# A recurrent token mixer and a token MLP on one core: from two loops over batch and head pair to planned units of 256 tokens

## The chip, the cores and the metric

The kernel runs on one core of one Trainium2 chip. The metric is the device time of one execution in microseconds (us); the number compared is the median of the runs. The core has TensorE (matrix products, into PSUM), VectorE, ScalarE, GpSimd and SyncE, and 16 transfer (DMA) engines. In the profile they are PE (with PEld for the loading of its stationary operand), DVE, ACT, POOL and SP.

## The reference

Inputs are fp32: r, k, v, w of shape batch 4, heads 8, tokens 768, head width 48; u of 8 x 48; and three small matrices. The first part is a recurrence per batch and head with a 48 x 48 state, the second mixes the tokens of a batch.

```python
for t in range(S):
    cur = einsum('bhd,bhe->bhde', u * kt, vt)
    y[:, :, t] = einsum('bhd,bhde->bhe', rt, state + cur)
    state = wt[..., None] * state + einsum('bhd,bhe->bhde', kt, vt)
x = y as (B, S, 384)                      # heads side by side
wq = x @ w_q; wk = x @ w_k                # 384 -> 64
W_tok = 64 ** -0.5 * einsum('bsd,btd->bst', wq, wk)
out = relu(einsum('bst,btd->bsd', W_tok, x)) @ w_out
```

Both kernels cut the recurrence into chunks of 128 tokens. In a chunk the decays become exponentials of running sums of logarithms of w; the tokens of a chunk act on each other through a masked 128 x 128 product per head, earlier chunks through the state. Both compute the mixing as wq (wk^T x), so that no 768 x 768 matrix arises.

## The kernel before

There are two loops: over the 4 batches, and within a batch first over 4 head pairs (`prep`), then over 6 chunks of 128 tokens (the scan), then the mixer. The order of instructions on each engine is that of the text; a tile framework adds the waits, and tiles with several buffers let a batch run into the next.

`prep` loads w, k, r and v of one head pair for all 768 tokens (four transfers of 288 KB on SP's queue, in pieces of 192 bytes, three buffers each). ScalarE takes the logarithm (`logw`, L144), TensorE sums along the tokens by triangular matrices (`cw`), ScalarE takes two exponentials (`ecwx`, L151, and `emcw`, L158), VectorE and GpSimd multiply r and k by them (`RdS`, L166, and `KdS`, L168). TensorE transposes both into `psT`, VectorE copies that to `RKT` (L177). Products `A` of 48 rows follow per chunk and head, and VectorE masks them into `AmB` (L188). The diagonal term with u is two products on GpSimd (`uk`, L195 and L196), a sum on VectorE (L198) and a product on GpSimd (`Vd`, L199). The scan makes a new state per chunk (`Sn`, then `SB`, L238) and the output `Y`, to which VectorE adds `Vd` (`X`, L250); each second chunk is transposed into `XT` (ScalarE copy, L260). The mixer has `wk_s`, `wqT`, `Tps`, six `mps` with a relu on ScalarE (L288), and six `fps` with a copy on VectorE (`osb`, L296) and a store on SP's queue (L297).

PSUM tiles of the scan, of the mixer and of the column sums `ptp` (L162, made in `prep`) share one ring `m` of two buffers:

```python
def mtile(shape, dtype, name):
    return ps.tile(shape, dtype, name=name, tag="m", bufs=2)
```

All matrix products go through the helper at L53, so that TensorE's instructions have line 54.

Of the kernel before, what the change touches and what calls it, by code (L numbers as in the profile page):

```python
# [18 lines left out]
def _rep(ap, axis, n):  # L19
    a = [list(x) for x in ap.ap]  # L20
    a.insert(axis, [0, n])
    return dataclasses.replace(ap, ap=a)
# [3 lines left out]
def kernel(  # L26
# [14 lines left out]
    C = 128  # L41
    NCH = S // C
# [5 lines left out]
    scale = 1.0 / math.sqrt(DH)  # L48

    MU = -0.13468  # L50
    LN_SCALE = math.exp(-MU)

    def mm(o, l, rr, start=True, stop=True, sgc=True, trans=False):  # L53
        nc.tensor.matmul(o, l, rr, start=start, stop=stop,  # L54
                         skip_group_check=sgc, is_transpose=trans)
# [4 lines left out]
    U128 = consts.tile([C, C], BF16, tag="U128")  # L60
    make_upper_triangular(nc, U128, 1.0, diag=True)
    US128 = consts.tile([C, C], BF16, tag="US128")
    make_upper_triangular(nc, US128, 1.0, diag=False)
    ID128 = consts.tile([C, C], BF16, tag="ID128")
    make_identity(nc, ID128)
    ones = U128[:, C - 1:C]

    iota0 = consts.tile([C, 1], mybir.dt.int32, tag="iota0")
    nc.gpsimd.iota(iota0, pattern=[[0, 1]], base=0, channel_multiplier=1)
    iota1 = consts.tile([C, 1], mybir.dt.int32, tag="iota1")  # L70
    nc.gpsimd.iota(iota1, pattern=[[0, 1]], base=1, channel_multiplier=1)
    bias_px = consts.tile([C, 1], F32, tag="bpx")
    bias_mi = consts.tile([C, 1], F32, tag="bmi")
    bias_c = consts.tile([C, 1], F32, tag="bc")
    nc.scalar.activation(bias_px, iota0, ACT.Copy, bias=0.0, scale=MU)
    nc.scalar.activation(bias_mi, iota1, ACT.Copy, bias=0.0, scale=-MU)
    nc.gpsimd.memset(bias_c, MU * C)

    NB = 3
    LW = []
    RdS = []
    for i in range(NB):
        t = consts.tile([C, NCH, C], BF16, name=f"logw{i}", tag=f"logw{i}")
        nc.gpsimd.memset(t, 0.0)
        LW.append(t)
        t = consts.tile([C, NCH, C], BF16, name=f"RdS{i}", tag=f"RdS{i}")
        nc.gpsimd.memset(t, 0.0)
        RdS.append(t)  # L90
    KdS = []
    PT = []
    for i in range(2):
        t = consts.tile([C, NP, NCH, C], BF16, name=f"KdS{i}", tag=f"KdS{i}")
        nc.vector.memset(t, 0.0)
        KdS.append(t)
        t = consts.tile([C, NCH, H], F32, name=f"pt{i}", tag=f"pt{i}")
        nc.vector.memset(t, 0.0)
        PT.append(t)

    u1 = consts.tile([1, DM], F32, tag="u1")
    ubc = consts.tile([C, DM], F32, tag="ubc")
    wq_sb = consts.tile([128, NK, DH], BF16, tag="wq")
    wk_sb = consts.tile([128, NK, DH], BF16, tag="wk")
    wout_sb = consts.tile([128, NK, DM], BF16, tag="wo")
    wq_f = consts.tile([128, NK, DH], F32, tag="wqf")

    ld = ctx.enter_context(tc.tile_pool(name="ld", bufs=3))
    hw = ctx.enter_context(tc.tile_pool(name="hw", bufs=3))
    bt = ctx.enter_context(tc.tile_pool(name="bt", bufs=2))  # L110
    sm = ctx.enter_context(tc.tile_pool(name="sm", bufs=3))
    ps = ctx.enter_context(tc.tile_pool(name="ps", bufs=1, space=bass.MemoryType.PSUM))
    xpool = ctx.enter_context(tc.tile_pool(name="xpool", bufs=2))
    msb = ctx.enter_context(tc.tile_pool(name="msb", bufs=2))
    mout = ctx.enter_context(tc.tile_pool(name="mout", bufs=4))

    def mtile(shape, dtype, name):
        return ps.tile(shape, dtype, name=name, tag="m", bufs=2)

    def prep(b, hp, AmB, RKT, VB, Vd, ptp):  # L120
        n = b * NP + hp
        wG = ld.tile([C, 2 * NCH, D], F32, name="wG", tag="wG")
        kG = ld.tile([C, 2 * NCH, D], F32, name="kG", tag="kG")
        rG = ld.tile([C, 2 * NCH, D], F32, name="rG", tag="rG")
        vG = ld.tile([C, 2 * NCH, D], F32, name="vG", tag="vG")
        for ap, tl in ((w, wG), (k, kG), (r, rG), (v, vG)):
            nc.sync.dma_start(out=tl, in_=ap[b, ds(hp * 2, 2)].rearrange(  # L127
                "h (c p) d -> p (h c) d", p=C))
        if n == 0:
            nc.sync.dma_start(out=u1, in_=u.rearrange("h d -> (h d)"))  # L130
            nc.gpsimd.partition_broadcast(ubc, u1)

        def hcd(t):
            return t.rearrange("p (h c) d -> p h c d", h=2)

        def chd(t):
            return t.rearrange("p (h c) d -> p c h d", h=2)

        def pad(t):
            return t.rearrange("p c (h x) -> p c h x", h=2)[:, :, :, 0:D]  # L140

        logw = LW[n % NB]
        for hh in range(2):
            nc.scalar.activation(logw[:, :, ds(hh * 64, D)],  # L144
                                 wG[:, ds(hh * NCH, NCH)], ACT.Ln,
                                 bias=0.0, scale=LN_SCALE)
        cw1 = ps.tile([C, 2, 512], F32, name="cw1", tag="cw")
        for hh in range(2):
            mm(cw1[:, hh, 0:NCH * D], US128, logw[:, :, ds(hh * 64, D)])
        ecwx = hw.tile([C, 2, NCH, D], BF16, name="ecwx", tag="ecwx")  # L150
        nc.scalar.activation(ecwx.rearrange("p h c d -> p h (c d)"),  # L151
                             cw1[:, :, 0:NCH * D], ACT.Exp,
                             bias=bias_px, scale=1.0)
        cw0 = ps.tile([C, 2, 512], F32, name="cw0", tag="cw")
        for hh in range(2):
            mm(cw0[:, hh, 0:NCH * D], U128, logw[:, :, ds(hh * 64, D)])
        emcw = hw.tile([C, 2, NCH, D], BF16, name="emcw", tag="emcw")
        nc.scalar.activation(emcw.rearrange("p h c d -> p h (c d)"),  # L158
                             cw0[:, :, 0:NCH * D], ACT.Exp,
                             bias=bias_mi, scale=-1.0)  # L160
        for c in range(NCH):
            mm(ptp[:, hp, ds(c, 1)], logw[:, c], ones)  # L162
# [165 lines left out]
```

## Time and profile before

| | |
|---|---|
| median of 3 runs | 181.64 us (180.85 to 182.18) |
| profiled execution, its span | 182.1 us (no other time is given for it) |
| TensorE, weight loads | 121.0 us, 74.3 us |
| VectorE | 112.7 us |
| ScalarE | 74.0 us |
| GpSimd | 95.3 us |
| TensorE's granted clock, mean | 0.869 of full speed |
| moved by transfers | 24.23 MB in 104,000 packets |

The span runs from the first to the last instruction of the profiled execution. Busy time of an engine is the time in which it worked on at least one instruction; the rest it waited or had nothing left.

### The profile page before, as it was taken

What the parts mean: (1) busy time and instruction counts of PE and PEld (TensorE: products, weight loads), DVE (VectorE), ACT (ScalarE), POOL (GpSimd) and SP (SyncE); (2) the same over time, 40 slices, a digit from 0 to 9 for tenths busy, and PEclk for the clock granted to TensorE, in tenths of its full rate; (3) what the DMA queues carried; (4) which work ended last, traced back from release to release, by engine and by line L of the source; (5) the groups of instructions that cost most, each with busy time, mean ns of one, the idle gap of its engine ahead of it and who ended that gap; (6) DMA issues with size and microseconds to landing.
All of it is one profiled execution on the core that took longest, in us unless ns stands there. A gap on an engine that the chain in (4) does not pass through costs nothing.

```text
span 182.1 us, 3121 instructions
## 1 busy us (share of the span) xinstructions
PE 121.0 (66%) x1200; PEld 74.3 (41%) x1200; DVE 112.7 (62%) x156; ACT 74.0 (41%) x140; POOL 95.3 (52%) x86
## 2 busy tenths in 40 slices
PE   0152178130698787966988986688888964787791
PEld 0121045010465653343765533465564243565240
DVE  6011147469889977644799778179996553744042
ACT  3175473310045446066346461944456232022620
POOL 8410599999728976406993954379586202000000
PEclk9999999999999997585599999657999697557969
DMA  7999999999999300399999908999940240000024
GB/s 127 186 188 187 187 185 158 196 215 157 169 187 168 67 4 2 142 236 200 190 178 191 166 13 237 235 168 200 185 73 0 86 150 27 0 5 0 0 81 178
DMA packets 104000, 24.23 MB, mean 133 GB/s; under 512 B 100529, under 2 KB 103986, under 8 KB 103986
## 3 DMA queue, kind: packets, MB, share of 16 engines
q1 hardware_dynamic: 103186, 23.70, 76.7%
q0 software_dynamic: 800, 0.34, 1.5%
q8 instruction: 9, 0.15, 0.4%
q14 instruction: 5, 0.04, 0.1%
HBM read 19.66 MB, written 4.72 MB: 134 GB/s over the span
## 4 chain that ended last, share of the span: by engine, by line
PE 25%; DVE 23%; issue 18%; POOL 12%; ACT 7%; DMA 7%; SPq 6%; POOLq 1%; ACTq 0%; DVEq 0%
DVE RdS L166 6%; PE psT L54 6%; DVE X L250 5%; SPq L127 5%; DVE RKT L177 5%; POOL uk L196 4%; DMA wG<-in_w_dram 3%; ACT XT L260 3%; POOL uk L195 3%; PE cw L54 3%; POOL Vd L199 3%; PE wq_ps L54 2%; PE fps L54 2%; DVE AmB L188 2%; PE Tps L54 2%
## 5 line engine op out<-in xcount | busy, mean ns | idle before, releaser
L168 POOL TENSOR_TENSOR KdS<-kG,emcw 128x576 bf16<-128x576 f32 x16 | 22.2, 1388 | 41.5 <-ACT emcw L158 33.2
L188 DVE TENSOR_TENSOR AmB<-A,US 128x768 bf16<-128x768 f32 x32 | 30.4, 950 | 5.7 <-PE A L54 4.4
L166 DVE TENSOR_TENSOR RdS<-rG,ecwx 128x576 bf16<-128x576 f32 x16 | 20.8, 1298 | 20.2 <-ACT ecwx L151 14.6
L177 DVE COPY RKT<-psT 128x1536 bf16<-128x1536 bf16 x16 | 15.3, 953 | 19.4 <-PE psT L54 19.3
L195 POOL TENSOR_TENSOR uk<-kG,ubc 128x576 f32<-128x576 f32 x16 | 24.0, 1499 | 0.0
L196 POOL TENSOR_TENSOR uk<-uk,rG 128x576 f32<-128x576 f32 x16 | 23.6, 1476 | 0.6
L199 POOL TENSOR_TENSOR Vd<-VB,diag 128x576 bf16<-128x576 bf16 x16 | 18.7, 1172 | 8.4 <-ACT VB L170 6.2
L54 PE MATMUL A<-RKT 48*128 48x128 bf16 x192 | 17.5, 263 | 7.0 <-DVE RKT L177 4.2
L144 ACT ACTIVATE logw<-wG 128x288 bf16<-128x288 f32 x32 | 12.4, 435 | 23.7 <-PE ptp L54 11.3
L151 ACT ACTIVATE ecwx<-cw,bias_px 128x576 bf16<-128x576 f32 x16 | 11.9, 741 | 24.6 <-PE cw L54 24.5
L54 PEld LDWEIGHTS <-KdS 128*128 128x128 bf16 x176 | 16.1, 123 | 13.7 <-POOL KdS L168 9.9
L54 PEld LDWEIGHTS <-RKT 48*128 48x128 bf16 (+1 forms) x272 | 13.6, 108 | 19.6 <-issue 9.3
L54 PE MATMUL fps<-wout_sb,mixT 128*128 128x384 bf16 x72 | 19.7, 418 | 1.7 <-ACT mixT L288 1.2
L296 DVE COPY osb<-fps 128x384 f32<-128x384 f32 x24 | 13.0, 554 | 12.4 <-PE fps L54 12.2
L54 PE MATMUL cw<-logw,US 128*128 128x288 bf16 x32 | 10.5, 365 | 13.4 <-ACT logw L144 12.9
L260 ACT COPY XT<-xt_ps 128x768 bf16<-128x768 bf16 x12 | 9.6, 799 | 21.4 <-PE xt_ps L54 21.4
L158 ACT ACTIVATE emcw<-cw,bias_mi 128x576 bf16<-128x576 f32 x16 | 11.9, 742 | 11.3 <-PE cw L54 11.2
L54 PE MATMUL psT<-ID,RdS 128*128 128x128 bf16 x96 | 11.4, 272 | 7.5 <-DVE RdS L166 7.5
L54 PE MATMUL cw<-logw,U 128*128 128x288 bf16 x32 | 9.7, 386 | 8.4 <-ACT ecwx L151 8.4
L54 PE MATMUL psT<-ID,KdS 128*128 128x128 bf16 x96 | 12.7, 277 | 2.8 <-POOL KdS L168 2.8
L170 ACT CAST VB<-vG 128x576 bf16<-128x576 f32 x16 | 10.7, 666 | 7.8 <-DMA vG<-in_v_dram 7.7
L54 PE MATMUL Sn<-VB,KdS 128*128 128x96 bf16 x80 | 9.9, 238 | 5.4 <-POOL KdS L168 5.4
(53 smaller groups left out, 181.1 us busy)
## 6 DMA issues: line engine op xcount, KB each, us to landing
wG<-in_w_dram SPq DMA_DIRECT2D x16, 288.0 KB, 5.6
kG<-in_k_dram SPq DMA_DIRECT2D x16, 288.0 KB, 5.3
rG<-in_r_dram SPq DMA_DIRECT2D x16, 288.0 KB, 5.6
vG<-in_v_dram SPq DMA_DIRECT2D x16, 288.0 KB, 5.6
out_dram<-osb SPq DMA_DIRECT2D x24, 192.0 KB, 1.9
wout_sb<-in_moe_w_out_dram POOLq DMA_DIRECT2D x1, 288.0 KB, 4.8
wq_f<-in_moe_w_q_dram SPq DMA_DIRECT2D x1, 96.0 KB, 4.6
wk_sb<-in_moe_w_k_dram POOLq DMA_DIRECT2D x1, 48.0 KB, 4.6
```

The source lines that it names most:

```text
L54: nc.tensor.matmul(o, l, rr, start=start, stop=stop, skip_group_check=sgc, is_transpose=trans)
L144: nc.scalar.activation(logw[:, :, ds(hh * 64, D)], wG[:, ds(hh * NCH, NCH)], ACT.Ln, bias=0.0, scale=LN_SCALE)
L151: nc.scalar.activation(ecwx.rearrange("p h c d -> p h (c d)"), cw1[:, :, 0:NCH * D], ACT.Exp, bias=bias_px, scale=1.0)
L166: nc.vector.tensor_tensor(pad(Rd), chd(rG), ecwx.rearrange("p h c d -> p c h d"), ALU.mult)
L168: nc.gpsimd.tensor_tensor(pad(Kd), chd(kG), emcw.rearrange("p h c d -> p c h d"), ALU.mult)
L177: nc.vector.tensor_copy(RKT[:, hp], psT[:, :, 0:NCH * C])
L188: nc.vector.tensor_tensor(AmB[:, ds(hp * 2, 2), ds(g * NG, NG)], A[:, :, 0:NG * C].rearrange("p h (c t) -> p h c t", c=NG), _rep(_rep(US12 ...
L195: nc.gpsimd.tensor_tensor(uk, hcd(kG), _rep(ubs, 2, NCH), ALU.mult)
L196: nc.gpsimd.tensor_tensor(uk, uk, hcd(rG), ALU.mult)
L199: nc.gpsimd.tensor_tensor(Vd[:, :, ds(hp * 2, 2)], VB[:, :, ds(hp * 2, 2)], _rep(diag.rearrange("p h c -> p c h"), 3, D), ALU.mult)
L260: nc.scalar.copy(XT[:, :, ds((c - 1) * C, 2 * C)], tp)
L296: nc.vector.tensor_copy(osb, fps)
```

## The change

The work is cut into 12 units, each of 256 tokens of one batch over all 8 heads. A unit is a list of some 50 steps, each with an engine, a booked duration, a rank, the steps it comes after and the buffer it fills. A scheduler in the kernel's text (`Plan.order`) plays these through at build time, with at most three transfers queued and PSUM as eight banks that are given out and taken back, and writes the steps in the order in which they came to start. The ranks are a unit number times 100 plus written-out offsets (`OFF`, `DEL`); a table (`ENG`) says per unit which of ScalarE (A), VectorE (D) and GpSimd (P) does a copy or product.

The parts change as well. A load brings 256 tokens of all heads in one transfer (393 KB, pieces of 384 bytes: two neighbouring tokens lie in one partition). k and r are cast to bf16 (`k16`, `r16`) and transposed by TensorE as they are; the running sums come out transposed (`cw`), and the exponentials `en` and `ep` are applied after the transposes: `RT` on VectorE out of PSUM, `KT` on VectorE or GpSimd. `kb` and `kd` turn `KT` back for the state. The diagonal term is a VectorE product `qT`, eight TensorE products with u as two columns (`dps`), a small copy (`dd`), and `Vd` on GpSimd. V is cast on GpSimd with the token pairs still side by side (`v16`); four transfers within SBUF put it in chunk order (`VB`). Masks take 1024 columns at a time. Copies of the mixer take a unit at a time: `xts`, `qks`, relu, `os`. The output is stored once a unit, 256 tokens. In the first and the last unit some steps are split in halves, and in the last the store of the first half is issued by ScalarE. Products of a zero tile stand at the start (9, and 26 as filler steps) and before the last batch's mixing (16).

The diff, cut to its core:

```diff
...
+    def add(self, eng, dur, rank, fn, after=(), fill=None, read=(), lag=100, mode=0,
+            behind=None, leave=0):
...
+    def dma(self, issue, dur, rank, fn, after=(), fill=None, read=()):
+
+        i = self.add("SP", issue, rank, fn, after, fill, read, lag=0)
+        m = self.add("DQ", dur, 0, self.nothing, [i], lag=0)
+        return i, self.add(f"L{m['n']}", 1950, 0, self.nothing, [m], lag=0)
...
+        ready = [s for s in self.steps if not left[s["n"]]]
+        running, done, eng_free, now = [], [], {}, 0
+        mode = queued = 0
+        while ready or running:
+            ready.sort(key=lambda s: (s["rank"] - self.stick * (s["eng"] == "PE"
+                                                                and s["mode"] == mode), s["n"]))
+            started = True
+            while started:
...
+                    if s["behind"] is not None and "start" not in s["behind"]:
+                        continue
+                    if ready_at[s["n"]] > now or eng_free.get(s["eng"], 0) > now:
+                        continue
+                    if s["eng"] == "SP" and queued >= 3:
+                        continue
...
+    U = 2 * C
+    NU = S // U
...
+    PS = ps.tile([C, 4096], F32, name="PS", tag="PS")
...
+    def load(b, i, tl, ap):
+        nc.sync.dma_start(
+            out=view(tl, 0, [[D2, H], [1, D2]]),
+            in_=ap[b, :, ds(i * U, U)].rearrange("h (p j) d -> p h (j d)", j=2))
...
+    for _ in range(9):
+        mm(PS[:, ds(0, 512)], Z[:, ds(0, C)], Z)
...
+    ENG = dict(k16="AAAAAPPPPPPP", r16="DADPPADPPPPA", KT="PDPDPPPPPPPP", kd="DAAADDDADAAA",
+               xts="ADDDDAADDDAA", qks="AADAAADAAAAA", rl="AAAAAAAAAAAA", os="AAAAAAAAAAAD",
+               dd="DADDDDDDDAAA", ks="AAAAAAAAAADA")
+    DEL = dict(load=[-2909, -1987, -122, 0, 5, 4, 16, 68, 52, 0, 4, 229],
...
+               os=[-209, -40, -196, 108, 0, 0, -5, -37, -26, 82, -198, -60],
...
+    kinds = {"os": NOS, "SB": 3}
+    for name in ("wg", "rg", "kg", "vg"):
+        kinds[name] = NB
+    for name in ("lw", "r16", "k16", "ep"):
+        kinds[name] = 2
+    for name in ("en", "ks", "qT", "RT", "KT", "ptm", "v16", "VB", "dd", "Vd", "AM0", "AM1", "KD", "XT"):
+        kinds[name] = NS
+    kinds["MX"] = 4
...
+    def warm(count, dur, after=()):
+
+        def f():
+            mm(stile(F32, "warm"), Z[:, ds(0, C)], Z)
+        for _ in range(count):
+            s_ = plan.add("PE", dur, 1 << 20, f, after, fill="s", lag=0)
+            plan.reads(s_, s_, True)
...
+        def f_cw():
+            t["cw"] = cw = wtile("cw")
+            for hp in range(NP):
+                for j in range(2):
+                    for c in range(2):
+                        mm(cw[:, ds(c * 512 + hp * C, C)],
+                           lw[ds(c * 64, 64), ds(j * 512 + hp * 128, 128)],
+                           CM[ds(c * 64, 64), ds(j * C, C)],
...
+            def f_en(cs=cs):
+                nc.scalar.activation(sb("en", [C, 1024])[:, cols(cs, 512)],
+                                     t["cw"][:, cols(cs, 512)], ACT.Exp, bias=0.0, scale=-1.0)
...
+        def f_qT():
+            nc.vector.tensor_tensor(sb("qT", [C, 1024]), t["rT"], t["ks"], ALU.mult)
...
+                nc.vector.tensor_tensor(
+                    view(sb("RT", [C, 1024]), cs[0] * 512, [[C, n4], [64, 2], [1, 64]]),
+                    view(t["rT"], cs[0] * 512, [[C, n4], [64, 2], [1, 64]]),
+                    view(ep, cs[0] * NP * EW, [[EW, n4], [66, 2], [1, 64]]), ALU.mult)
...
+        def f_vm():
+            x = sb("VB", [C, 2 * DM])
+            for c in range(2):
+                for j in range(2):
+                    nc.sync.dma_start(out=x[ds(j * 64, 64), ds(c * DM, DM)],
+                                      in_=t["v16"][ds(c * 64, 64), ds(j * DM, DM)])
+        issue, land = plan.dma(1700, 1200, rank("vp", n), f_vm, [g["v16"].by[0]], "VB")
+        plan.reads(land, g["v16"].first, True)
...
+                    mm(x[:, ds(c * H + hp * 2, 2)], t["qT"][:, ds((c * NP + hp) * C, C)],
+                       UB[:, ds(hp * 2, 2)], start=(c == 0 and hp == 0), stop=True)
...
+                    view(t[f"A{c}"], 0, [[C, 8], [1, C]]),
+                    view(US, 0, [[0, 8], [1, C]]), ALU.mult)
...
+                nc.vector.scalar_tensor_tensor(
+                    view(X["t"], (2 * i + c0) * DM, [[DM, ncs], [1, DM]]),
+                    view(t["y"], c0 * 512, [[512, ncs], [1, DM]]), gx,
+                    view(t["Vd"], c0 * DM, [[DM, ncs], [1, DM]]), ALU.mult, ALU.add)
...
+            if end and ii == 0:
+                warm(16, 215, Tall)
...
+            first = plan.add("PE", 4700, -1 << 20, plan.nothing)
+            warm(26, 215, [first])
...
+        for s in plan.order():
+            now["step"] = s
+            s["fn"]()
...
```

## Rows read from the trace of the kernel before

**Rows 1.** The page, busy time of each engine, share of the span and instructions.

```profile
PE 121.0 (66%) x1200; PEld 74.3 (41%) x1200; DVE 112.7 (62%) x156; ACT 74.0 (41%) x140; POOL 95.3 (52%) x86
```

**Rows 2.** Busy time by stage: PE, PEld, DVE, ACT, POOL, granted clock, transfer share, GB/s.

```profile
0.00:25.00 25.00, 6.42 (x44) 3.52 (x45) 5.07 (x7) 11.24 (x21) 11.04 (x24) 1.00 1.30 176
...
82.50:116.85 34.35, 27.67 (x301) 17.50 (x301) 25.91 (x38) 17.89 (x35) 22.14 (x16) 0.85 0.97 174
...
151.40:182.10 30.70, 20.66 (x174) 12.45 (x173) 12.49 (x21) 6.53 (x12) 1.27 (x1) 0.72 0.11 39
```

**Rows 3.** The chain that ended last: start, length, what.

```profile
82.50 1.28 POOL KdS L168
...
116.85 1.29 POOL KdS L168
```

**Rows 4.** Waits: who for whom, us in total, times, longest.

```profile
POOL KdS L168 <- ACT emcw L158: 33.2, 10, 8.4
...
ACT logw L144 <- PE ptp L54: 11.3, 2, 6.0
...
PE ptp L54 <- DVE osb L296: 2.7, 3, 1.4
```

**Rows 5.** Two stretches by window: loads at the full, output stores alone.

```profile
50.00:58.00 8.00, 7.27 (x95) 5.47 (x94) 7.35 (x13) 3.83 (x7) 3.58 (x3) 1.00 1.45 188
178.00:179.00 1.00, 0.45 (x3) 0.06 (x1) 1.00 (x2) 0.00 (x0) 0.00 (x0) 1.00 0.90 329
```

**Rows 6.** ScalarE's groups of instructions: count, busy, mean ns of one, idle before.

```profile
L144 ACT ACTIVATE logw<-wG 128x288 bf16<-128x288 f32 x32 | 12.4, 435 | 23.7 <-PE ptp L54 11.3 <-issue 7.1 <-DMA wG<-in_w_dram 5.2
...
L151 ACT ACTIVATE ecwx<-cw,bias_px 128x576 bf16<-128x576 f32 x16 | 11.9, 741 | 24.6 <-PE cw L54 24.5
...
L170 ACT CAST VB<-vG 128x576 bf16<-128x576 f32 x16 | 10.7, 666 | 7.8 <-DMA vG<-in_v_dram 7.7
...
L260 ACT COPY XT<-xt_ps 128x768 bf16<-128x768 bf16 x12 | 9.6, 799 | 21.4 <-PE xt_ps L54 21.4
...
L275 ACT CAST wqT<-wq_ps 64x384 bf16<-64x384 f32 x8 | 3.8, 472 | 6.3 <-PE wq_ps L54 6.3
```

**Rows 7.** VectorE's groups of instructions.

```profile
L188 DVE TENSOR_TENSOR AmB<-A,US 128x768 bf16<-128x768 f32 x32 | 30.4, 950 | 5.7 <-PE A L54 4.4 <-PE mps L54 1.0
...
L177 DVE COPY RKT<-psT 128x1536 bf16<-128x1536 bf16 x16 | 15.3, 953 | 19.4 <-PE psT L54 19.3
...
L238 DVE TENSOR_TENSOR SB<-Sn,pt 128x384 bf16<-128x384 f32 x20 | 11.0, 548 | 2.6 <-PE Sn L54 2.5
```

**Rows 8.** Line 166 on VectorE: shortest, median and longest ns.

```profile
L166 DVE TENSOR_TENSOR RdS<-rG,ecwx x16: 748/759/6481, 10.5 to 150.1; 128x576 bf16<-128x576 f32 x16
```

**Rows 9.** GpSimd's groups of instructions.

```profile
L199 POOL TENSOR_TENSOR Vd<-VB,diag 128x576 bf16<-128x576 bf16 x16 | 18.7, 1172 | 8.4 <-ACT VB L170 6.2 <-DVE diag L198 2.2
...
L86 POOL MEMSET logw<- 128x768 bf16 x3 | 2.2, 738 | 0.0
```

**Rows 10.** TensorE in order of time: two slow groups, then two fast ones.

```profile
50.66 0.85 PE L54 MATMUL psT<-ID,RdS 128*128 128x128 bf16 x6
51.30 0.85 PE L54 MATMUL psT<-ID,KdS 128*128 128x128 bf16 x6
...
94.33 0.51 PE L54 MATMUL psT<-ID,RdS 128*128 128x128 bf16 x6 [0.23 <-DVE RdS L166]
94.67 0.28 PE L54 MATMUL psT<-ID,KdS 128*128 128x128 bf16 x2
```

**Rows 11.** The start in order of time: the first load's issue, its first user.

```profile
0.73 0.43 SPq L127 DMA_DIRECT2D wG<-in_w_dram  x1
...
4.46 0.78 ACT L144 ACTIVATE logw<-wG 128x288 bf16<-128x288 f32 x2 [1.96 <-DMA wG<-in_w_dram]
```

**Rows 12.** The end in order of time: VectorE's last add.

```profile
165.82 0.56 DVE L250 TENSOR_TENSOR X<-Y,Vd 128x384 bf16<-128x384 f32 x1
```

**Rows 13.** SP's transfer queue: what it waited for, us, times, longest.

```profile
SPq L297 <- DVE osb L296: 66.4, 19, 25.7
```

More of the change, by code (lines that the diff above doesn't have):

```diff
@@ new lines @@
+    ID16 = const([C, C], BF16, "ID16")
+    Z = const([C, 512], BF16, "Z")
+    US = const([C, C], F32, "US")
+    CM = const([C, 2 * C], BF16, "CM")
+    MB = const([C, 2], F32, "MB")
+    pos0 = const([C, 1], mybir.dt.int32, "pos0")
+    pos1 = const([C, 1], mybir.dt.int32, "pos1")
+    gx = const([C, 1], F32, "gx")
+    gv = const([C, 1], F32, "gv")
+    nc.vector.memset(Z, 0.0)
+    for _ in range(9):
+        mm(PS[:, ds(0, 512)], Z[:, ds(0, C)], Z)
+    nc.vector.memset(uT, 0.0)
+    for hh in range(2):
+        nc.scalar.dma_start(out=view(uT, hh, [[2, NP], [1, 1]], p0=hh * 64, pn=D),
+                            in_=dataclasses.replace(u, offset=hh * D,
+                                                    ap=[[1, D], [D2, NP], [1, 1]]))
@@ new lines, in stile, with took, copy @@
+    def stile(dtype, name):
+        x = PS[:, ds(now["step"]["buf"]["bank"][0] * 512, 512)]
+        return x if dtype == F32 else x.bitcast(dtype)
+    def took(eng, cols, half=False, by=False):
+        if eng == "A":
+            return (265 if by else 180) + int(cols * 0.83)
+        if eng == "P":
+            return 140 + int(cols * 1.94)
+        return (210 if by else 150) + int(cols * (0.52 if half else 1.04))
+    def copy(eng, o, i, by=None):
+        if eng == "A":
+            if by is None:
+                nc.scalar.copy(o, i)
+            else:
+                nc.scalar.activation(o, i, ACT.Copy, bias=0.0, scale=by)
+        elif by is None:
+            nc.vector.tensor_copy(o, i)
+        else:
+            nc.vector.tensor_scalar_mul(o, i, by)
@@ new lines, in f_ub @@
+    def f_ub():
+        nc.gpsimd.tensor_copy(UB, uT)
+    for n in range(B * NU):
+        if n % NU == 0:
+            batch = {"X": {}, "qks": [], "wq": [], "xs": []}
+        if n == 0:
+            wl = plan.dma(1500, 2500, 105, f_wld)[1]
+            first = plan.add("PE", 4700, -1 << 20, plan.nothing)
+            warm(26, 215, [first])
+            state["ub"] = plan.add("POOL", 200, 12, f_ub)
+            state["wts"] = plan.add("POOL", 1800, 120, f_wcast, [wl])
+        unit(n, state, batch)
@@ L301 @@
+    with tc.manual_schedule():
+        for s in plan.order():
+            now["step"] = s
+            s["fn"]()
 _INS = ['r', 'k', 'v', 'w', 'u', 'moe_w_q', 'moe_w_k', 'moe_w_out']
```

800 lines of the change are left out of this document (581 added, 219 removed).

## The prediction

> **What bounds the kernel now.** I read the page's busy shares first: no engine is over 66% busy [rows 1]. So the time is lost between engines, and the next view is the busy time by stage [rows 2]. In the first 25 us TensorE works 6.4 us and VectorE 5.1, while the transfers run full. A middle stretch of 34.35 us, one batch long, holds at most 27.7 us of work on any engine. In the last 30.7 us GpSimd has one instruction, VectorE is 41% busy and TensorE 67%. The chain of waits shows that this middle stretch is a batch's period: the same GpSimd product stands in it at 82.50 and 116.85 [rows 3]. The waits say why. GpSimd's key product waits 33.2 us in all for the exponential, up to 8.4 us once; the logarithm ahead of it waits 11.3 us for the products into `ptp`; and `ptp` waits for the last output copies, whose PSUM tiles are of the same ring `m` [rows 4]. The next batch's preparation is thus held behind the mixer of this one. Three limits, then: 25 us until a whole batch's first data are in, three periods of 34 us at about 80% of the fullest engine, and an end that nothing overlaps. The profiled span, 182.1 us, is all that is given of that execution; it lies 0.5 us above the median of 181.64, and I sum against it.
>
> **The change, part by part.** All of the schedule goes, so I sum each engine anew and then ask which stands longest and how tightly a fixed order can pack it. There are 12 units. Durations at new widths are lines through the rows at old ones.
>
> *Transfers.* Loads stay 18.9 MB, but 48 transfers in pieces of 384 bytes replace 64 in pieces of 192. At the full stretch 188 GB/s were moved in 192-byte pieces, so one of 16 transfer engines takes 192 x 16 / 188 = 16.3 ns a piece; output rows of 1536 bytes came to 329 GB/s at 0.90 busy, 67 ns a piece [rows 5]. No row has 384 bytes. The bounds are 16.3 ns (a piece costs the same) and 32.6 ns (bytes cost the same): 50 to 100 us for 49,152 pieces. I take the line between the two rows, 23.6 ns, since it is nearest to the shorter: 1.51 us a load, 72.5 us in all. Stores: 16 x 67 ns = 1.1 us a unit, 12.9 in all. The V put is new, four transfers within SBUF of 64 x 768 bytes a unit; the line gives 38 ns a piece, 0.6 us a unit, 7 us in all, with bounds of 188 and 329 GB/s at 7 to 13 us. Sum 93 us, but the start needs one unit instead of a batch.
>
> *The Trainium skill against the V put.* No row here has a transfer over 64 partitions. The Trainium skill, SBUF — State Buffer, section Door 1: The DMA port swizzle, says that partitions 0 to 63 reach no more ports than 0 to 31, so that half the rate is to be had. By that the V put would be 14 us, and the transfers' sum 100; by the rows it is 7.
>
> *ScalarE.* PSUM copies took 472 ns at 384 columns and 799 at 768: 0.851 a column on a foot of 145. The exponential took 741 at 576, the logarithm 435 at 288, the cast 666 at 576 [rows 6]. New: 24 exponentials of 1024 at 741 + 448 x 0.851 = 1122 ns, 26.9 us, and 1 us for the split ones; 12 logarithms of 768 at 843, 10.1; 16 copies of 1024 (`ks` 11, `kd` 5) at 1016 and 2 of 512, 17.5; 8 casts of 768 at 829, 6.6; 26 of 768 (`xts`, relu, `os`) at 799, 20.8; 16 of 384 at 472, 7.6; small ones 1. Sum 91.5 us, where ScalarE was busy 74: it takes over output copies and bf16 casts from VectorE and GpSimd.
>
> *VectorE.* 950 ns at 768 and 548 at 384 make 1.047 a column from fp32 PSUM; the bf16 copy of 1536 took 953, or 0.525 a column on the same foot [rows 7]. New: 24 masks of 1024 at 1.218 us, 29.2; 12 adds of 768, 11.4; 20 state products, 11.0; 24 products of bf16 out of PSUM (`qT`, `RT`) at 0.684, 16.4; copies of `xts`, `kd`, `r16`, `ks`, `KT`, `qks`, `dd` by the same lines 15.8. Sum 84 us. The reduction for the diagonal is gone (its work is 8 two-column products on TensorE). The `qT`/`RT` rate is not in the trace: no two-input instruction there reads bf16 PSUM. Bounds are 0.684 and 1.219 us; I take the first, by the bf16 PSUM copy. A gain beside it: the product of two SBUF inputs on VectorE has a minimum of 748 ns, a median of 759 and a maximum of 6481 [rows 8]; the row doesn't say what held the longest, so I count no gain for it. Two `KT` products of that kind remain.
>
> *GpSimd.* The bf16 product of 576 took 1172 ns, 2.03 a column [rows 9]: ten `KT` of 1024 20.8 us, twelve `Vd` of 768 18.8. The 25 casts of 768 have no row; a memset of 768 at 738 ns is below them, a product of 768 at 1560 above; I take 0.9, nearer to the one-stream row: 22.5 us (18 to 39). With small ones 68 (64 to 85), where it was 95. It is not the bound by any of these.
>
> *TensorE.* Six transposes begin 0.34 us before the next group at the fast pace, 57 ns each, and 0.64 at the slow one, 107 each [rows 10]. A unit has some 15,300 columns of products, 4,100 of them in pairs on half the rows; at 57/128 ns a column and the pairs at half, 5.9 us a unit, 71 in all; at the slow pace 133. The fillers (9 + 26 at the start, 16 before the last mixing) stand where TensorE has nothing else, so I cost them at nothing; were they in the way, one is 512 columns, 0.23 us, 12 us for all.
>
> *Waits added.* SP's one queue now holds loads, V puts and stores. A V put waits for GpSimd's cast, and behind it stand the loads of later units; three buffers a tensor give two units of room, some 15 us at the forecast pace, so I cost this at nothing in the middle. The first unit pays it in full, and it is hidden there by ScalarE's own work on units 0 and 1.
>
> **The sum.** ScalarE is longest. Its first input was issued at 0.73 and used at 4.46 [rows 11]; the larger transfer makes that 4.9. Then 91.5 us of work. The first unit's pipeline leaves about 3 us empty (two turns by way of TensorE). The end after the last add is a chain: before it took 16.3 us, from 165.82 to 182.1 [rows 12], for six chunks one after another; now half-units go through five products and five copies (0.4 us each and a hand-over), then a store, about 9 us, of which ScalarE works 2.5: 6.5 empty. For holes between: at best none, at worst the 25% that VectorE is idle in the middle stretch [rows 2], a third of the work, 30 us; I take 8%, 7.3 us, near the low end because the wait on ring `m` that makes those holes is gone and preparation is interleaved with mixing. What is late next, I expect, is ScalarE emptying PSUM, and TensorE waiting for its banks. 4.9 + 91.5 + 3 + 6.5 + 7.3 = 113, beside 182.1. Transfers as a check: the last load lands at 3 + 72.5 + 11/12 of 20 = 94, then 8 us to the last add and 9 to the end: 111. I say 114. The holes give 106 to 136, and 104 if exponentials go by the plain copies' line.
>
> **Rivals.**
> 1. *VectorE becomes the bound.* If `qT` and `RT` go at 1.047 ns a column, as the masks do, VectorE has 84 + 24 x 0.535 = 97 us, starts when r, the third load, lands (8), and loses 6.5 at the end and 8%: 119. For it: every two-input product from PSUM in the rows goes at 1.047; against: those were fp32. The Trainium skill, VectorE: DVE Perf Modes, section The perf-mode tier table, lists tensor_tensor with any PSUM operand in the slowest mode, and copies from PSUM in up to the doubled one. The trace agrees for the copy (0.525 a column) and for fp32 products; bf16 products it doesn't show. Chance 15%, 112 to 128.
> 2. *Bytes cost, not pieces.* Loads at 188 GB/s take 100 us, stores 14, V puts 13; last load at 127, end at 144. For it: the transfers were full at that rate; against: 329 GB/s with longer rows. Chance 8%, 128 to 150.
> 3. *The slow clock.* TensorE is granted 0.85 of full speed in the middle stretch now, at 80% busy; were the slow pace to hold throughout, its 133 us + 8 at the start + 6 at the end make 147. Against: its gaps become shorter. Chance 7%, 130 to 150. Fillers that lift nothing cost only the first units, a few us.
> 4. *Slower: the transfer queue closes a round trip.* Were SP's head-of-line wait to reach the loads, each unit would go load (3.7 and three more at 1.5), cast 0.9, V put 3.6, products and add 2: 14.7 us, 12 x 14.7 + 9 = 185. It decides from a period of 14.3 us on. For it: SP's queue already waits 66.4 us for output copies, 25.7 once [rows 13]; against: three buffers. Chance 3%.
>
> **How the numbers follow.** The forecast as told has 67%. 104 to 136 holds it, rival 1 and a little of 2 and 3; what is left out is under 2 in 10. A measurement can tell about 1%. Only rival 4 is slower: 3%; within 1%: 1%; faster: 96%.
>
> **What would show it.** ScalarE and VectorE over 75% busy with about 91 and 84 us; `qT`/`RT` at 0.68 (rival 1: 1.2); loads at 250 to 270 GB/s in full stretches (rival 2: 188); granted clock near 1.0 past the start; first add at about 15 us, end 9 after the last add. It is wrong if holes pass a third, or if a planned order meets durations far from these and waits at queue heads.

## The result and the profile after

The changed kernel takes 121.33 us (120.95 to 121.46, 4 runs), beside 181.25 us (179.94 to 182.18) for the kernel before in the same measurement: a ratio of 0.669, with a 95% interval of 0.665 to 0.673. Measured again on another occasion it took 119.32 us (118.42 to 120.69), 0.657 [0.651, 0.663]. The two differ by 2 us, so a difference of 2 us between kernels that did not run side by side is none here. The forecast was 114 us, with 104 to 136. The profiled execution took 121.27 us, 1.7 us more than its span. (Ratios leave out executions over 1.5% above the fastest of their kernel, among them one of the kernel without fillers that took 272.09 us, with products of 384 columns at 894 ns for 326, so that no line of that profile is shown.)

The page of the changed kernel: the busy time of each engine, the transfers in 40 slices of 3 us, and the share of the main transfer queue (packets, MB, share of 16 engines).

```profile
PE 102.9 (86%) x1486; PEld 70.9 (59%) x1486; DVE 85.9 (72%) x140; ACT 82.9 (69%) x117; POOL 67.3 (56%) x84
...
DMA  2999995999889895988994949899759881127064
GB/s 56 307 321 325 335 242 130 248 275 248 226 189 266 222 318 117 324 227 218 317 308 113 331 109 326 274 282 323 188 144 325 256 303 32 40 100 263 0 229 169
...
q1 hardware_dynamic: 58128, 26.55, 79.8%
```

Against [rows 1] ScalarE works more (82.9 for 74.0), VectorE and GpSimd less (85.9 for 112.7, 67.3 for 95.3), and all in 119.6 us instead of 182.1. TensorE's 102.9 holds 14.7 of filler products, and ends that are modelled. The transfers reach 320 to 335 GB/s where they run full, beside 188 in [rows 5], yet fall to 109 to 189 in seven slices between 18 and 90 us: something holds them up again and again.

The busy time in stretches of 5 us, by the columns of [rows 2]: the start, two stretches where loads run full, one with a V put in it (40 to 45, the put from 41.84 to 45.54) and the one behind it, one that lies between two puts (85.1 to 90.1), and the end.

```profile
0.00:5.00 5.00, 3.77 (x9) 1.34 (x10) 3.68 (x14) 1.87 (x2) 2.50 (x15) 1.00 0.64 155
5.00:10.00 5.00, 5.00 (x47) 2.68 (x46) 2.11 (x10) 4.44 (x10) 1.60 (x5) 1.00 1.17 321
10.00:15.00 5.00, 5.00 (x70) 3.03 (x67) 2.84 (x6) 3.90 (x5) 3.46 (x5) 1.00 1.14 330
...
40.00:45.00 5.00, 4.11 (x79) 3.16 (x79) 3.69 (x8) 2.71 (x4) 4.48 (x4) 1.00 1.13 311
45.00:50.00 5.00, 5.00 (x62) 3.48 (x59) 4.97 (x7) 4.25 (x7) 3.41 (x4) 1.00 0.78 203
...
85.10:90.10 5.00, 4.63 (x106) 3.81 (x101) 4.30 (x8) 2.09 (x4) 4.42 (x5) 1.00 0.55 138
...
105.00:110.00 5.00, 4.61 (x48) 2.93 (x44) 2.02 (x5) 3.07 (x7) 0.00 (x0) 1.00 0.44 159
110.00:115.00 5.00, 5.00 (x27) 2.46 (x26) 2.46 (x5) 2.58 (x6) 0.00 (x0) 1.00 0.15 55
115.00:119.60 4.60, 3.30 (x17) 1.37 (x14) 0.88 (x2) 0.48 (x1) 0.00 (x0) 1.00 0.64 231
```

The start of [rows 2], 25 us with TensorE at 6.4, is gone. From 85.1 to 90.1 the transfers carry 138 GB/s, and in that stretch ScalarE works 2.09 us of 5. What ended such idle time stands in the waits (who for what, us in total, times, longest):

```profile
ACT lw L469 <- DMA wg<-in_w_dram: 13.2, 9, 2.8
POOL v L563 <- DMA vg<-in_v_dram: 10.6, 9, 3.0
POOL Vd L593 <- DMA VB<-v: 5.8, 4, 2.4
```

None of the waits of [rows 4] is left; the largest three are for transfers. The logarithm, ScalarE's first step of a unit, waits 13.2 us for w. The load it waits for is late because of what stands ahead of it in SyncE's queue, in order of time (start, length, count):

```profile
38.21 0.53 SPq L243 DMA_DIRECT2D wg<-in_w_dram  x1
38.84 0.53 SPq L243 DMA_DIRECT2D kg<-in_k_dram  x1
39.46 1.09 SPq L243 DMA_DIRECT2D rg<-in_r_dram  x1
40.60 1.14 SPq L243 DMA_DIRECT2D vg<-in_v_dram  x1
41.84 3.70 SPq L571 DMA_DIRECT2D VB<-v  x4
45.65 0.53 SPq L243 DMA_DIRECT2D wg<-in_w_dram  x1
...
49.32 3.01 SPq L571 DMA_DIRECT2D VB<-v  x4
52.46 1.15 SPq L243 DMA_DIRECT2D wg<-in_w_dram  x1
...
103.45 13.21 SPq L829 DMA_DIRECT2D out_dram<-os  x8
```

Read the first column and the second together: each entry begins where the one before ends. The queue has hardly a free moment up to 98.6 us, and the four transfers of a V put hold it for 3.0 to 3.7 us of a unit's 7.5 in these rows (41.84 to 49.32), for 2.4 to 4.4 over all twelve, 38 us in sum. The lengths are not issue alone: by the profile's list of waits, loads and puts on SyncE waited 19 us in all for buffers and casts, mostly inside these entries. The loads behind the put at 41.84 are issued in 0.53 us each, as is the pair at 38.21, and the next two in 1.1. During the put the transfers still run full on what was queued before it (1.13 from 40 to 45), and behind it they fall to 0.78 (45 to 50). I read 0.53 as the issue into a queue that has drained, and 1.1 as the pace of full transfers.

The landing of the put has a part too. The chain that ended last goes, near its end, through two landings that `Vd` waited for (start, length):

```profile
84.47 3.46 DMA VB<-v
...
92.60 3.38 DMA VB<-v
```

### The profile page after: what moved, and what is told of

Same layout as the page of the kernel before. It is cut to its first block, busy times and chain, and to the rows that moved or that the text cites. A ratio compares the mean times of both kernels' runs of the same rounds, so it can differ in the third digit from the quotient of the medians.

```text
span 119.6 us, 3729 instructions
## 1 busy us (share of the span) xinstructions
PE 102.9 (86%) x1486; PEld 70.9 (59%) x1486; DVE 85.9 (72%) x140; ACT 82.9 (69%) x117; POOL 67.3 (56%) x84
## 5 line engine op out<-in xcount | busy, mean ns | idle before, releaser
L611 DVE TENSOR_TENSOR AM<-PS,US 128x1024 bf16<-128x1024 f32 x24 | 29.0, 1220 | 4.8 <-PE PS L204 3.5
L593 POOL TENSOR_TENSOR Vd<-VB,dd 128x768 bf16<-128x768 bf16 (+1 forms) x14 | 18.0, 1292 | 8.1 <-DMA VB<-v 5.8
L549 POOL TENSOR_TENSOR KT<-ks,en 128x1024 bf16<-128x1024 bf16 (+1 forms) x12 | 21.6, 1802 | 0.7 <-ACT ks L374 0.7
L469 ACT ACTIVATE lw<-wg 128x768 bf16<-128x768 f32 x12 | 10.2, 847 | 13.2 <-DMA wg<-in_w_dram 13.2
L204 PE MATMUL PS<-Z 128*128 128x512 bf16 x51 | 14.7, 434 | 1.2 <-DVE uT L260 1.2
L500 ACT ACTIVATE en<-PS 128x1024 bf16<-128x1024 f32 (+1 forms) x14 | 12.6, 900 | 2.4 <-PE PS L204 1.7
L698 DVE SCALAR_TENSOR_TENSOR X<-PS,gx,Vd 128x768 bf16<-128x768 f32 (+1 forms) x13 | 12.3, 952 | 2.7 <-PE PS L204 2.4
L657 DVE TENSOR_TENSOR SB<-PS,ptm 128x384 bf16<-128x384 f32 x20 | 11.0, 552 | 3.0 <-PE PS L204 3.0
L204 PE MATMUL PS<-wo,MX 128*128 128x384 bf16 x72 | 13.2, 326 | 0.0
L506 ACT ACTIVATE ep<-PS 128x1024 bf16<-128x1024 f32 (+1 forms) x14 | 12.9, 920 | 0.0
L374 ACT COPY ks<-PS 128x1024 bf16<-128x1024 bf16 x11 | 11.1, 1013 | 0.8 <-PE PS L204 0.7
```

Source lines behind the costliest of these rows:

```text
L204: nc.tensor.matmul(o, l, rr, start=start, stop=stop, skip_group_check=True, is_transpose=trans)
L374: nc.scalar.copy(o, i)
L469: nc.scalar.activation(view(lw, 0, [[64, H], [512, 2], [1, D]]), view(wg, 0, [[D2, H], [D, 2], [1, D]]), ACT.Ln, bias=0.0, scale=math.exp( ...
L500: nc.scalar.activation(sb("en", [C, 1024])[:, cols(cs, 512)], t["cw"][:, cols(cs, 512)], ACT.Exp, bias=0.0, scale=-1.0)
L506: nc.scalar.activation(view(ep, cs[0] * NP * EW + 66, [[EW, NP * len(cs)], [-65, 2], [1, 64]]), t["cw"][:, cols(cs, 512)], ACT.Exp, bias=0 ...
L549: e.tensor_tensor(sb("KT", [C, 1024])[:, cols(cs, 512)], t["ks"][:, cols(cs, 512)], t["en"][:, cols(cs, 512)], ALU.mult)
```

## The experiments

The changed kernel's own time is 121.3 and 119.3 us by the two measurements; ratios are against the kernel before on the same chip.

**The V put left out.** `Vd` and the mixing products read `v16` itself, whose tokens stand in the order of the load and not of the chunks, so V's rows are permuted. `v16` has four buffers in this run, as many as `v16` and `VB` had together.

```diff
-            x = sb("VB", [C, 2 * DM])
...
-                    nc.sync.dma_start(out=x[ds(j * 64, 64), ds(c * DM, DM)],
-                                      in_=t["v16"][ds(c * 64, 64), ds(j * DM, DM)])
+            t["VB"] = t["v16"]
```

> The four transfers that put V in chunk order are left out in every unit, and the products read V as GpSimd cast it, in the order of token pairs (so V's rows stand in another order). The order of all other steps is kept. Theory A: SP's queue sets the middle. In the changed kernel a V put holds it for about 3.0 us a unit and loads stand behind it; without the puts 12 x 3.0 = 36 us of the queue are free, and the time falls until the transfers themselves or ScalarE's 83 us of work with its holes set it: 108 to 114 us. Theory B: the fixed order of the compute engines sets it, and the puts lie beside other work: 120 to 122 us. Under A ScalarE's logarithm waits for loads under 6 us in all (13.2 in the changed kernel); under B that wait stays.

Measured: 111.06 us (110.65 to 111.31), 0.609 [0.604, 0.614], in A's range. SyncE's queue, in order of time:

```profile
43.59 1.25 SPq L243 DMA_DIRECT2D rg<-in_r_dram  x1
44.94 1.15 SPq L243 DMA_DIRECT2D vg<-in_v_dram  x1
46.17 1.13 SPq L243 DMA_DIRECT2D wg<-in_w_dram  x1
47.40 1.10 SPq L243 DMA_DIRECT2D kg<-in_k_dram  x1
48.59 2.45 SPq L243 DMA_DIRECT2D rg<-in_r_dram  x1
```

and the logarithm's wait in the list of waits of the same kernel:

```profile
ACT lw L469 <- DMA wg<-in_w_dram: 2.1, 1, 2.1
```

Loads now follow each other at the pace of the transfers and wait for buffers instead (2.45); the wait for w falls from 13.2 us to 2.1. The put costs 8 to 10 us of the time.

**The V put made twice**, the second time into a tile that nobody reads.

```diff
+            x2 = sb("VB2", [C, 2 * DM])
...
+                    nc.sync.dma_start(out=x2[ds(j * 64, 64), ds(c * DM, DM)],
+                                      in_=t["v16"][ds(c * 64, 64), ds(j * DM, DM)])
```

> Each of the four V transfers of a unit is issued twice, the second time into a tile that nobody reads; no product waits for it. Theory A (SP's queue time): 12 x 3.0 us more in the queue, most of it on the path: 148 to 157 us. Theory C (the bytes of the puts): 2.4 MB more at the 320 GB/s of full stretches, 7 us: 125 to 129 us. Theory B (hidden beside the compute engines' order): 121 to 124 us.

Measured: 147.84 us (147.37 to 148.31), 0.811. The queue shows the price of one such transfer:

```profile
42.34 0.59 SPq L574 DMA_DIRECT2D VB<-v  x1
42.98 0.59 SPq L572 DMA_DIRECT2D VB<-v  x1
43.61 0.59 SPq L574 DMA_DIRECT2D VB<-v  x1
```

Starts lie 0.64 us apart, so 48 more are 30.5 us of queue; the time rose by 26.5. That is 0.16 us below the low end of what the queue theory said, and far from the 125 to 129 of the theory that counts bytes. The rival that the transfers themselves are slow, and hold the queue up, falls too: in the second half of this put the issues keep their pace while the transfers are at 0.38 of a full share and 89 GB/s:

```profile
44.50:46.20 1.70, 1.70 (x24) 1.50 (x21) 0.02 (x1) 1.70 (x3) 0.86 (x2) 0.50 0.38 89
```

The granted clock of this run was 0.883, where the changed kernel had 0.986 and 0.938, so a part of the 26.5 may be TensorE's; this was not separated.

**V loaded in chunk order**, by four loads of 64 partitions in pieces of 192 bytes (`load_v`, not shown), and no put. GpSimd casts V without a change of order, and `v16` has four buffers.

```diff
-                                   lambda tile_=tile_, ap=ap: load(b, i, tile_, ap), fill=name)
+                                   lambda tile_=tile_, ap=ap, ld=(load_v if name == "vg" else load):
+                                   ld(b, i, tile_, ap), fill=name)
...
-            x = sb("VB", [C, 2 * DM])
...
+            t["VB"] = t["v16"]
```

> One part undone: V comes from memory in chunk order, by four loads a unit of 64 x 8 pieces of 192 bytes, GpSimd casts it straight into the tile that the products read, and there are no transfers within SBUF; the result is the reference's. Theory A (SP's queue): per unit three loads at 1.2 us and four at about 0.6 take 6.0 us where four loads and the put took 7.4 to 7.8; 12 x 1.5 = 18 us are freed, of which the first 10 count until the next bound, 111 us, is met: 111 to 114. Theory D (what counts is the put's landing, 3.4 us between cast and product, not the queue's time): 111 as well, but then e8 should stay near 121. Theory C (bytes and pieces of transfers): the V load becomes 0.9 us a unit longer and the put's 0.6 goes: 121 to 125.

Measured: 116.39 us (115.64 to 117.19), 0.642 [0.635, 0.649]. Neither range holds it, A's by 2.4 us. The put and its wait are gone, but the four loads take 3.2 to 4.8 us of SyncE's queue for the 1.1 of one; the logarithm still waits 9.6 us for w, and now V itself is late:

```profile
POOL v L572 <- DMA vg<-in_v_dram: 13.5, 9, 4.0
```

**Pieces of 192 bytes for every load**, with the units, the put and the plan as they are.

```diff
-            out=view(tl, 0, [[D2, H], [1, D2]]),
-            in_=ap[b, :, ds(i * U, U)].rearrange("h (p j) d -> p h (j d)", j=2))
+            out=view(tl, 0, [[D, 2 * H], [1, D]]),
+            in_=dataclasses.replace(ap, offset=b * H * S * D + i * C * D,
+                                    ap=[[D, C], [S * D // 2, 2 * H], [1, D]]))
```

The tokens of a unit are then in chunk order for all tensors, and the put permutes V away from it.

> The loads move the same bytes in pieces of 192 bytes as in the kernel before, two token blocks of one partition being fetched apart (so tokens come in another order); the order of steps is kept. If pieces cost the same whatever their size, 98,304 of them at 16.3 ns on each of 16 engines are 100 us where the changed kernel spends 58 (1.21 us a load). Theory A, in which loads and puts share one queue one after another: 121 + 12 x 4 x 0.85 = 155 to 162 us. If the order of the compute engines set the time and the transfers had room: 121 to 135 us.

Measured: 150.43 us (149.83 to 151.02), 0.826. Below A's range by 4.6 us, but 15 above the upper end of the theory by which the order alone made the gain. Three windows of 20 us, with the transfers' share and GB/s in the last two columns:

```profile
20.00:40.00 20.00, 13.53 (x201) 10.65 (x201) 11.34 (x17) 10.99 (x15) 9.35 (x11) 0.74 1.05 201
40.00:60.00 20.00, 15.15 (x216) 11.90 (x217) 12.24 (x20) 11.09 (x14) 9.35 (x11) 0.74 0.86 169
60.00:80.00 20.00, 16.00 (x231) 11.62 (x230) 11.80 (x19) 12.52 (x16) 11.74 (x12) 0.91 1.06 188
```

At a full share 188 and 201 GB/s are moved, as in [rows 5], so the rate belongs to the piece. Of the 60 us that the change gained, the longer piece brings at most about half (29 us); without it the rest of the change, its units, engines and order together, gives 31. The granted clock fell to 0.74 in two of them, so part of the 29 may be TensorE's; this was not separated.

**No offsets in the plan**: every step of a unit has the unit's own rank, and the hand-set shifts of kinds of steps are zero.

```diff
-        return STEP * n + OFF[at] + (DEL[at][n] if at in DEL else 0)
+        return STEP * n
```

> The written-out offsets of the ranks are all zero, so that the scheduler takes steps by unit number and then as they become ready; all steps and their engines are as in the changed kernel. Theory A: the queue's work is the same, and the middle is set by it; only the start and the end suffer: 124 to 135 us. Theory B: the order is what the time comes from: 140 to 165 us.

Measured: 126.91 us (126.49 to 127.32), 0.697. In A's range; the shifts are worth 5.6 us against the one measurement of the changed kernel and 7.6 against the other, about a tenth of the gain.

**Two transfers for the put instead of four.** Half of V's blocks don't change partitions; GpSimd casts them straight into `VB`, and only the two that travel go by a transfer. `VB` has four buffers here instead of two; in the changed kernel SyncE's puts waited 1.3 us in two waits for `Vd`, the reader of `VB`, so the two more can't be worth the 4 us.

```diff
-            nc.gpsimd.tensor_copy(view(sb("v16", [C, 2 * DM]), 0, [[D, H], [DM, 2], [1, D]]),
-                                  view(vg, 0, [[D2, H], [D, 2], [1, D]]))
+            for c in range(2):
+                for j in range(2):
+                    o = sb("VB" if c == j else "v16", [C, 2 * DM])
+                    nc.gpsimd.tensor_copy(view(o, j * DM, [[D, H], [1, D]], p0=c * 64, pn=64),
+                                          view(vg, j * D, [[D2, H], [1, D]], p0=c * 64, pn=64))
...
-                for j in range(2):
-                    nc.sync.dma_start(out=x[ds(j * 64, 64), ds(c * DM, DM)],
+                j = 1 - c
+                nc.sync.dma_start(out=x[ds(j * 64, 64), ds(c * DM, DM)],
```

> Two of the four V transfers a unit are taken out: their partitions are the same on both sides, so GpSimd casts these blocks straight into place, in four casts of 64 partitions and 384 columns instead of one; the other two transfers stay, with their landing, and the result is the reference's. Theory A (queue time): 24 transfers x 0.64 us = 15 us less in SP's queue, until the next bound near 111: 111 to 115 us. Theory D (landing time): the landing stays, 119 to 122. A rival price: four casts cost GpSimd some 1.2 us a unit more, 14 us on 67; if GpSimd's place in the order counts, 116 to 120.

Measured: 115.19 us (114.46 to 115.88), 0.634 [0.627, 0.640], 0.2 us above A's range and below the others. A landing takes 3.3 us in the median where it took 3.4, so it isn't its length that was saved; but `Vd`, which waited 5.8 us for it, waits 1.0 now, since the last of two is issued sooner than the last of four. This run alone doesn't part the issue from the landing. The page of this version, busy time of each engine:

```profile
PE 102.2 (90%) x1486; PEld 70.6 (62%) x1486; DVE 86.4 (76%) x140; ACT 83.1 (73%) x117; POOL 79.9 (70%) x120
```

Its list of waits, the logarithm's:

```profile
ACT lw L469 <- DMA wg<-in_w_dram: 4.5, 3, 2.4
```

The wait for w falls from 13.2 to 4.5 us, though GpSimd works 12.6 us more (79.9): four casts of 64 partitions at some 505 ns take the place of one of 825.

**The same, with the two travelling blocks cast first.**

```diff
-            for c in range(2):
-                for j in range(2):
-                    o = sb("VB" if c == j else "v16", [C, 2 * DM])
+            for far in (1, 0):
+                for c in range(2):
+                    j = c ^ far
+                    o = sb("VB" if c == j else "v16", [C, 2 * DM])
```

> The version with two transfers (115.2 us), with GpSimd casting the two blocks that travel before the two that stay. The put can then be issued some 1.0 us earlier in each unit (two casts of 505 ns). If the put's release is what SyncE's queue waits for in that version (9.8 us in four waits on the cast), the time falls by 1 to 3 us, to 112 to 114; if something else sets the pace of the unit, it stays within 0.7 us of 115.2.

Measured: 115.09 us (114.98 to 116.38, 6 runs), 0.636 [0.632, 0.640]: no change. SyncE's wait for the cast is 9.3 us in four waits, as before; putting the cast earlier by 1 us doesn't move the unit's pace, so neither the cast nor the landing sets it in this version. On the same chip the changed kernel took 119.32, so the two-transfer version is 4.2 us faster than it, and faster than both kernels of this case.

**The put issued by ScalarE.**

```diff
-                    nc.sync.dma_start(out=x[ds(j * 64, 64), ds(c * DM, DM)],
+                    nc.scalar.dma_start(out=x[ds(j * 64, 64), ds(c * DM, DM)],
```

> All four transfers of V's put are issued by ScalarE's instruction stream and not by SyncE's; their bytes, shapes and number stay. Theory A (it is the time that the issue takes on the issuing stream): SyncE's 12 x 2.6 us = 31 us go away, and ScalarE, 82.9 us busy of 119.6 and idle for 36.7, takes 48 x 0.6 = 29 us instead. If ScalarE pays them in full its own sum is 83 + 29 = 112 and with the start and the end (some 15 us) the time is 124 to 132; if an issue costs ScalarE next to nothing, 110 to 114. In both cases SyncE's loads follow each other every 1.1 to 1.2 us and the logarithm's wait for w shrinks from 13.2 us to under 5. Theory C (it is the copy's own transfer through SBUF, wherever it is issued): 120 to 123, with the wait for w as before.

Measured: 122.61 us (120.99 to 123.29), 0.674 [0.667, 0.681], 3.3 us above the unedited kernel on that chip. The issues on ScalarE's stream, shortest, median and longest ns, first and last start:

```profile
L571 ACTq DMA_DIRECT2D VB<-v x48: 468/607/1748, 9.3 to 95.6; - x48
```

The logarithm's wait in this kernel:

```profile
ACT lw L469 <- DMA wg<-in_w_dram: 2.7, 2, 2.3
```

What its loads on SyncE waited for longest:

```profile
SPq L243 <- DMA VB<-v: 22.5, 7, 6.0
```

The time lies in C's range, but C said that the wait for w stays, and it fell to 2.7 us. An issue takes the same 0.6 us on ScalarE's stream as on SyncE's; 48 x 0.607 = 29 us on top of 82.5 busy make 112 of a span of 120.8, and the time is 1.4 us below A's 124. And a wait came that neither theory had: by the profile SyncE's loads stood 22.5 us in seven waits behind the landing of puts that another stream issued. So the issue's time goes with the issuing stream, as A says; that the landing is free is not shown by this run, and no time was gained.

**The fillers left out**, but for the first; and then only the 16 ahead of the last mixing.

```diff
-    for _ in range(9):
+    for _ in range(1):
...
-                warm(16, 215, Tall)
+                pass
...
-            warm(26, 215, [first])
```

> The products of the zero tile are left out, all but the first one; they go into no output. If the fillers at the start lift TensorE's clock ahead of the first unit, the first transposes go at 107 ns instead of 57 until TensorE has been busy for a while: some 100 products x 0.05 = 1 to 5 us later at the start, of which the load queue hides most in the middle: 121 to 125 us. If the fillers stand in the way anywhere, 119 to 121.

> Only the 16 zero products of the last batch's mixing are left out. The last twelve of them ran from 115.54 to 118.29 us in the changed kernel's trace, after the last output product and beside the last copies and stores, so they can end the execution no earlier than the last store lands: 120.8 to 121.4 us, or 0.3 to 0.8 us less if TensorE's last product was what the end waited for. If the clock falls without them, 122 to 123.

Measured: 119.40 us without nearly all, 0.660 [0.652, 0.667]; 120.35 us without the last 16 (all four from 119.89 to 123.92), 0.664 [0.654, 0.673]. Both intervals overlap those of the unedited kernel's measurements: the fillers make no difference that can be told here. The first time lies in the range for fillers that stand in the way, but so does the unedited kernel's own 119.32, so it says nothing for that. The kernel without the last 16 had a granted clock of 0.971, beside 0.986 and 0.938 in the two profiles of the changed kernel.

**The changed kernel again**, beside the last two.

> The changed kernel itself, unedited, beside the two others on the same chip: 120.8 to 121.6 us by every theory. It is there so that the differences of a few us are read on one chip.

Measured: 119.32 us (118.42 to 120.69), below what was expected. Its waits tell the same story: 10.3 us for w, 8.4 for v, 5.3 for the put.

## Why the prediction came out as it did

The time lay 7 us above the forecast and inside the range; the sum hid two errors of opposite sign, 8.6 us too much and 16 too little, so that it came this near is in part luck. By ScalarE, as the prediction summed it, in the same terms:

| term | forecast | measured | from |
| --- | --- | --- | --- |
| start | 4.9 | 3.1 | idle to 5.0; the first logarithm starts at 4.41 |
| ScalarE's work | 91.5 | 82.9 | page |
| first unit's pipeline | 3 | 1.7 | idle from 5 to 15 |
| holes between | 7.3 | 23.4 | idle from 15 to 105: 90 less the rest of the work, 66.6 |
| end | 6.5 | 8.5 | idle from 105 to 119.6 |
| outside the span | none | 1.7 | 121.3 less 119.6 |
| sum | 113 | 121.3 | |

**The holes.** The step that failed is in "Waits added": "three buffers a tensor give two units of room, some 15 us at the forecast pace, so I cost this at nothing in the middle". I counted the put's bytes on the transfer engines (7 us, hidden) and its wait for the cast, but not that its four issues take time in the queue in which the loads stand. They take 48 x 0.64 = 31 us there. With two issues a unit the time falls by 4, with none by 8 to 10, with eight it rises by 26.5. I read the small step down and the large step up as those of a queue that is just at the limit, with ScalarE, VectorE and TensorE next below it; that next bound was not tested. Of the 16 us by which the holes outgrew the forecast the put thus explains 8 to 10, and the cause of the other 6 stays open. The plan itself has the put too short: it books 1.7 us for the four issues and 0.45 for a load's, where the trace has 3.2 and 1.0 in the mean, waits included; what truer figures would have given was not tried. Nor came what I expected to be late next, ScalarE emptying PSUM and TensorE waiting for its banks: the three largest waits are for transfers. The Trainium skill, Perfetto Trace Analysis, section What "DMA-bound" means, counts an issuing engine's queue that is solid with transfers as a bound of its own, beside the transfer engines; this trace agrees, with entries end to end from 38.21 to 52.46. The "8%" itself was a choice inside 0 to 30 us, and 23.4 is in its upper part. [Rows 13] and rival 4 named the right place, the head of SyncE's queue, but I priced it as a closed round trip of 14.7 us a unit, from waits. From the first put to the last the period is 7.7 us in the mean, and issues fill more of it than waits do.

**ScalarE's work**, 8.6 us too much by the page. By form, the groups that I had sized by lines through [rows 6] and [rows 7] (instruction, count, busy, mean ns, idle before):

```profile
L611 DVE TENSOR_TENSOR AM<-PS,US 128x1024 bf16<-128x1024 f32 x24 | 29.0, 1220 | 4.8 <-PE PS L204 3.5 <-issue 1.1
...
L374 ACT COPY ks<-PS 128x1024 bf16<-128x1024 bf16 x11 | 11.1, 1013 | 0.8 <-PE PS L204 0.7
...
L506 ACT ACTIVATE ep<-PS 128x1024 bf16<-128x1024 f32 x10 | 10.4, 1039 | 0.0
...
L563 POOL CAST v<-vg 128x768 bf16<-128x768 f32 x12 | 9.9, 825 | 10.7 <-DMA vg<-in_v_dram 10.6
...
L531 DVE TENSOR_TENSOR qT<-PS,ks 128x1024 bf16<-128x1024 bf16 x12 | 8.2, 686 | 3.0 <-ACT ks L374 1.5 <-PE PS L204 1.5
...
L538 DVE TENSOR_TENSOR RT<-PS,ep 128x1024 bf16<-128x1024 bf16 x10 | 6.8, 683 | 0.2 <-ACT ep L506 0.2
```

The copies came as drawn (1013 for 1016). The exponentials take 1020 to 1039 where I had 1122 and 600 where they are split, 2.4 us less in all. Of the copies of 768 there are 22 on ScalarE where I counted 26 (the last batch shares its relu and output copies with VectorE), 3.2 us less, and 20 of 384 where I counted 16, 2.0 us more. With these and small ones ScalarE's rows sum to 90.4 us, close to the 91.5. Most of the 8.6 is something else: an instruction often starts before the one ahead of it has ended, and the page counts that time once, 82.9. Two in order of time, of which the second starts 0.11 us before the first ends:

```profile
6.74 0.59 ACT L500 ACTIVATE en<-PS 128x512 bf16<-128x512 f32 x1
7.22 0.60 ACT L506 ACTIVATE ep<-PS 128x512 bf16<-128x512 f32 x1
```

So the sizes were right and the step that set them end to end was not: 7.5 us overlap. VectorE's sum, 84, came to 85.9 busy (some 92 by its rows); GpSimd's, 68, to 67.3.

**The end.** The last add ends at 106.2 and the span at 119.6: 13.4 us where the prediction said "about 9". The step "now half-units go through five products and five copies" took one half-unit's chain for the whole. All three units of the last batch have their last products behind it:

```profile
105.06 1.14 DVE L698 SCALAR_TENSOR_TENSOR X<-PS,gx,Vd 128x384 bf16<-128x384 f32 x2 [2.41 <-PE PS L204]
...
110.21 2.36 PE L204 MATMUL PS<-qk,ts 128*128 128x256 bf16 x9
112.40 0.38 PE L204 MATMUL PS<-Z 128*128 128x512 bf16 x1
112.62 3.09 PE L204 MATMUL PS<-wo,MX 128*128 128x384 bf16 x18
```

**The transfers.** 23.6 ns for a piece of 384 bytes was drawn; at 320 to 335 GB/s a piece takes 16 x 384 / 330 = 18.6 ns, near to the 16.3 of the short one. By this rate the loads are 57 us of transfer time for 72.5. That a longer piece moves more was right: the run with short pieces is 29 us slower, with the clock's part in it as said.

**The rivals.** Rival 1 falls: a product with a bf16 PSUM input takes 683 to 686 ns at 1024 columns, as taken, not 1219; the rule of the Trainium skill that the prediction set beside it (VectorE: DVE Perf Modes, section The perf-mode tier table) doesn't hold for these rows, and the measurement decides. Rival 2 falls with 320 to 335 GB/s. For rival 3 the pace of the products is the surer sign, since the slow groups of [rows 10] at 50.66 stand in a stretch whose granted clock was 1.00 [rows 5]. In the changed kernel eight transposes that begin at 65.48 are followed at 65.93, 56 ns each; groups of eight go at the slow pace only from 29.92 to 32.03, 104 ns each, where the granted clock was 0.50, and its mean was 0.986. So rival 3 falls. Rival 4 is told above. Whether the V put's 64 partitions halve its rate, as by the Trainium skill (SBUF — State Buffer, section Door 1: The DMA port swizzle), no run isolates: doubling the put was paid at the price of its issues.

**The signs.** The rate of `qT` and `RT` and the clock came as said. ScalarE and VectorE stayed under 75% busy (69 and 72), the loads ran faster than 250 to 270 GB/s, the first add began at 19.9 us and not at about 15, and the end took 13.4 and not 9.

## What to carry to other kernels

Cost a transfer three times: its bytes, its landing, and its issue on the stream that issues it, and sum the issues of each stream over a unit of work, as for an engine. Of several small transfers ahead of a load, first drop those whose data could be written in place; here moving the issue to another engine's stream moved its price there. A planned order is only as good as the durations that it was given, so look in its trace first for the one queue without gaps.

## What the runs showed of the hardware

- Issuing one transfer within SBUF of 64 partitions x 768 bytes takes 0.59 us of SyncE's stream and 0.61 of ScalarE's. A load of 384 KB in 1,024 pieces took 0.45 as the first of the kernel, 0.53 behind the puts at 34.56 and 41.84, and 1.1 to 1.2 where loads follow one another; an output store took 0.33 at the least and 0.39 in the median.
- A product of two inputs, one of them bf16 in PSUM, goes at the pace of a bf16 PSUM copy: 683 ns for 1024 columns, where a PSUM input in fp32 took 1220.
- Pieces of 384 bytes moved 320 to 335 GB/s at a full share, pieces of 192 bytes 188 to 201: some 18.6 ns a piece on each of 16 engines beside 16.3, for twice the bytes.
- Zero products that keep TensorE busy at the start and before the last mixing changed nothing that can be measured.
